# Gated mix of sliding-window attention and a SwiGLU block: two tiles' gate and up products moved into the block products, and the inverses of the softmax sums moved into the last slots

## The chip, the cores and the metric

The kernel runs on one core of a Trainium2 chip. The metric is the device time of one execution in microseconds (us). TensorE (PE, with its weight loads PEld), VectorE (DVE), ScalarE (ACT) and GpSimd (POOL) compute; SyncE (SP), ScalarE and GpSimd start transfers, which sixteen DMA engines carry out. Each engine works through its instructions in the order in which the program wrote them; nothing reorders them here.

## The reference

```python
def _A_ref(x, wqkv, wo):              # S = 2048, D = 512, H = 32 heads of 16, W = 256
    qkv = (x @ wqkv).reshape(B, S, 3, H, Dh).transpose(2, 0, 3, 1, 4)
    scores = einsum("bhqd,bhkd->bhqk", q, k) * (Dh ** -0.5)
    mask = (i - j >= 0) & (i - j < W)
    p = softmax(where(mask, scores, -1e9)); o = einsum("bhqk,bhkd->bhqd", p, v)
    return o.transpose(0, 2, 1, 3).reshape(B, S, D) @ wo
def _B_ref(x, w_gate, w_up, w_down):  # F = 1792
    return (silu(x @ w_gate) * (x @ w_up)) @ w_down
g = sigmoid((x * gate_w).sum(-1))
return g * _A_ref(x) + (1 - g) * _B_ref(x)
```

All is float32. The kernel gets float32 accuracy out of TensorE by splitting each operand into a high half (`hi`, a cast on ScalarE) and a low half (`lo`, a subtraction on VectorE or GpSimd), and by three matmuls per product (`split`, L66; `mm3`, L76).

## The kernel before, in words

The work has four stages, and TensorE passes through them without a break.

**Values and block products (to L439).** First the inputs are loaded: `x` by chunks of 512 tokens and `wv`, alternately on SyncE's queue (L143 to L148). Then the value projection of all 16 token blocks (L209). Then `PAIRS` (L149): the query and key projections of two head groups at a time, as seven block products of a Strassen-Winograd scheme (`product`, L357) in place of eight, for both halves of the tokens (`a`). A pair is 7 x 2 x 6 = 84 matmuls of 128x512. Each result block is handed to `put_c` (L332), which splits it and writes it to DRAM (`xd`); `stack` (L317) reads it back in the layout that the scores need. `soon` puts a step off by a number of products.

**First scores (L629 to L656).** 64 ticks in which the row maxima of group 0 are found.

**Slots (L734 to L770).** 128 slots `t`, 16 for each of the 8 head groups `g`; each has four ticks `hd`, one a head. A tick runs one matmul of `stage1` (L533: scores of group g+1 for the row maxima, taken by VectorE, L547), one of `stage2` (L573: scores of group g, exponential on ScalarE, L586, masks on GpSimd, L588 and L591) and a number of steps of `stream` (L526). Two score banks each (`ps1`, `ps2`) lie between TensorE and VectorE or ScalarE. In the last group (from t = 112, `g7`) there is no `stage1`, and `stage2` runs two heads in every second tick. Every fourth slot, after its second tick, holds a value product (`av`, L596, up to 96 short matmuls), then `evacuate` (L613): ScalarE and VectorE copy its two banks, GpSimd adds and writes to `od`. The sum of the softmax comes out of the same product, as one more column.

`stream` computes gate and up of the SwiGLU block, 14 tiles of 128 columns with two products each: 28 `UNITS`, for each 48 steps. A step is two matmuls of 64 rows side by side (`lanes`, L476; `whole`, L500, for the first unit). A unit's four result blocks are copied by ScalarE (L516) and written to `raws` (L517); its weights are split by ScalarE and GpSimd (`prepare`, L296). 192 steps run beside the first scores, 1152 in the slots: 9 a slot. How many steps a tick gets is written out by hand (L754 and L762).

Single steps are attached to ticks by `at(k, ...)`, `later(n, ...)` and `spread`, with k = 4t + hd; they run at the end of their tick. So are placed: the gate (`gate_block`, L661: load a block of x, multiply and sum on VectorE nine ticks later; `gate_end`, L667); early loads of `wd` (L673); early loads and the silu of the first SwiGLU tiles (`tile_load`, L683; `tile_early`, L688; `tile_silu`, L700), for which the freed query and key slots serve (`pieces`).

**The tail (L772 to L954).** 56 tiles (four token chunks c of 14 tiles n): load gate and up from `raws` (`load_kept`), silu and product (`hidden`), halves (`halved`), 12 matmuls with `wd` (`step`). Beside it the attention output: `load_oc` reads the unnormalized heads of a chunk from `od`, `load_den` the softmax sums, `put_den` inverts them on VectorE and writes `rd`, `load_rd` reads the inverses back, spread over the heads' rows; `attn_step` divides, splits and multiplies by `wo`. In the tail of the kernel before, all four `load_den` stand at its beginning, `put_den` at tiles 9 to 12 of chunk 0, the reads of chunk 0 at tiles 10 to 13 and those of chunk c at its first four tiles. All of these transfers are GpSimd's. Chunk 0's division begins at tile 1 of chunk 1.

Of the kernel before, what the change touches and what calls it, by code (L numbers as in the profile page):

```python
# [33 lines left out]
def gated_mix(ctx, tc, xT, xn, wqk, wv, wo, wgu, wd, gw, out):  # L34
# [70 lines left out]
    UNITS = [("f", f, i) for f in range(NF) for i in range(2)]  # L105
# [37 lines left out]
    for k in range(NK):  # L143
        nc.sync.dma_start(xk(0, k), xT[0, k])
        nc.sync.dma_start(wvraw[k], wv[:, k])
# [3 lines left out]
    PAIRS = [(("p", g), ("p", g + 1)) for g in range(0, G, 2)]  # L149
    RW = {0: pair_fetch(PAIRS[0])}  # L150

# [297 lines left out]
    with ExitStack() as A:  # L449
# [207 lines left out]

        gwb = osb.tile([P, D], F32, name="gwb")
        nc.sync.dma_start(gwb, gw[None, :].to_broadcast([P, D]))

        def gate_block(b):  # L661
            t = osb.tile([P, D], F32, name="xn", bufs=2)
            nc.sync.dma_start(t, xn[b * P:(b + 1) * P])
            later(9, lambda: nc.vector.scalar_tensor_tensor(t, t, 1.0, gwb, op0=ALU.mult, op1=ALU.mult,
                                                            accum_out=gate[:, b:b + 1]))

        def gate_end():  # L667
# [3 lines left out]
            nc.vector.tensor_scalar(igate, gate, -1.0, 1.0, op0=ALU.mult, op1=ALU.add)  # L671

# [64 lines left out]

        for t in range(G * NB + 1):
# [5 lines left out]
            for hd in range(4):  # L744
# [9 lines left out]
                n = (2, 1, 2, 2)[hd] if values else (k + 1) * 9 // 4 - k * 9 // 4  # L754
# [15 lines left out]
        run(last_tile)  # L770

    with ExitStack() as B:  # L772
# [26 lines left out]

        DEN = wop.tile([P, NCH, P], F32, name="den")  # L800
        shares = od.rearrange("g (j e) s -> (g j) e s", e=32)[:, DH]

        def load_den(c):
            nc.gpsimd.dma_start(DEN[:, c], shares[:, c * CH:(c + 1) * CH].rearrange("h (q i) -> h q i", q=4))

        def put_den(c):
            nc.vector.reciprocal(DEN[:, c], DEN[:, c])
            nc.gpsimd.dma_start(rd[c].rearrange("h (q i) -> (h q) i", q=4), DEN[:, c])

# [99 lines left out]
        for c in range(NCH):  # L909
            load_den(c)  # L910
        GOT[0, 3] = GOT[3]
        loads = seq[4:]
# [3 lines left out]
        for c, n in seq[3:]:  # L916
# [5 lines left out]
            if c == 0:  # L922
# [5 lines left out]
                else:  # L928
# [5 lines left out]
                    if n >= 10:  # L934
                        load_oc(0, n - 10)
            elif n < 4:
                load_oc(c, n)
            if c == 0 and n >= 10:
                load_rd(0, n - 10)
            elif c and n < 4:  # L940
                load_rd(c, n)
# [47 lines left out]
```

## Time and profile before

| what | us |
|---|---|
| median of three runs (lowest, highest) | 835.11 (833.59, 836.22) |
| the profiled execution's own time | 835.55 |
| its span, first to last instruction | 833.8 |
| TensorE busy in it | 816.1 |
| value projection and head pairs end at | 127.45 |
| first slot begins at, last value product ends at | about 182, about 621 |

The profile is one execution as the chip's profiler took it. Busy time counts an engine's instructions; an engine off the critical path may idle for nothing. A row of a timeline gives start, duration, engine, line, operation, written and read tile and shape; brackets give the idle time before it and what ended that. Matmuls are pipelined, so their durations overlap; the distance between starts is what one costs.

### The profile page before, as it was taken

The numbers are of one execution on the slowest core, as the hardware profiler recorded it, in microseconds if no ns is written. First come the engines' busy times: TensorE is split into PE (matmuls) and PEld (weight loads), VectorE is DVE, ScalarE is ACT, GpSimd is POOL, SyncE is SP. The second block draws the span as 40 slices with busy tenths as digits, with TensorE's granted clock in tenths as the row PEclk, the third lists the DMA queues.
The fourth block names the chain that finished last, engine by engine and source line by source line (L and its number), as shares of the span: only waits on it lengthen the run. The fifth ranks groups of instructions, "written<-read, shape, count | busy, mean of one in ns | idle before, by whom it ended". The sixth has DMA issues, their size and how long they took to land.

```text
span 833.8 us, 20786 instructions
## 1 busy us (share of the span) xinstructions
PE 816.1 (98%) x7897; PEld 684.0 (82%) x7897; DVE 541.6 (65%) x1394; ACT 471.0 (56%) x953; POOL 398.7 (48%) x712
## 2 busy tenths in 40 slices
PE   8999999999999999999999999999999979999997
PEld 7888887998888888888888888888887768888886
DVE  5675534877868787778787777783477466365462
ACT  7454552246767676666666766676776433434341
POOL 5124468035656575656565665665734532123220
PEclk9999999999999999999999999999999979999999
DMA  8446668672555556466446543534559995685741
GB/s 292 151 161 242 227 253 290 222 225 94 178 164 179 174 179 204 136 202 209 149 167 192 175 159 130 191 107 146 204 191 361 256 220 160 190 263 167 220 146 51
DMA packets 80420, 158.94 MB, mean 191 GB/s; under 512 B 14912, under 2 KB 19392, under 8 KB 80320
## 3 DMA queue, kind: packets, MB, share of 16 engines
q1 hardware_dynamic: 70128, 130.32, 48.7%
q0 software_dynamic: 10192, 27.29, 10.2%
q8 instruction: 62, 1.02, 0.5%
q14 instruction: 38, 0.31, 0.1%
HBM read 92.80 MB, written 64.75 MB: 189 GB/s over the span
## 4 chain that ended last, share of the span: by engine, by line
PE 88%; DMA 5%; DVE 4%; POOL 1%; ACT 1%; issue 1%; SPq 0%; DVEq 0%; ACTq 0%; POOLq 0%
PE pa L489 17%; PE pb L489 17%; PE ps L608 9%; PE ps L545 6%; PE ps L584 5%; PE ps L82 5%; PE ps L81 5%; PE ps L80 4%; PE ps L371 4%; PE pa L371 3%; PE ps L209 3%; PE pb L371 3%; DVE ps L547 2%; PE pb L81 2%; PE pb L80 2%; DMA got<-raws 2%
## 5 line engine op out<-in xcount | busy, mean ns | idle before, releaser
L547 DVE CUSTOM_DVE_ANT_0 ps<-ps,mask 128x384 f32<-128x384 f32 (+2 forms) x512 | 272.6, 545 | 50.2 <-PE ps L545 24.0
L586 ACT ACTIVATE pt<-ps 128x384 f32<-128x384 f32 (+2 forms) x512 | 237.2, 478 | 83.0 <-PE ps L545 31.9
L584 PE MATMUL ps<-q,k 64*128 64x384 f32 (+2 forms) x512 | 165.5, 333 | 0.1
L545 PE MATMUL ps<-k,q 63*128 63x384 f32 (+2 forms) x512 | 159.2, 331 | 1.9 <-DVE mx L547 0.4
L588 POOL TENSOR_SCALAR_AFFINE_SELECT pt<-pt 128x256 f32<-128x256 f32 x256 | 107.0, 418 | 107.0 <-ACT pt L586 102.4
L545 PEld LDWEIGHTS ps<-k,q 63*128 63x128 f32 x512 | 88.9, 184 | 20.4 <-DVE mx L547 10.1
L584 PEld LDWEIGHTS ps<-q,k 64*128 64x128 f32 x512 | 93.1, 184 | 9.9 <-ACT pt L586 4.4
L489 PE MATMUL pb<-xhi,wh 64*128 64x512 f32 x432 | 98.8, 402 | 0.0
L489 PE MATMUL pb<-xlo,wh 64*128 64x512 f32 x432 | 97.2, 393 | 0.0
L489 PE MATMUL pa<-xhi,wh 64*128 64x512 f32 x432 | 96.7, 399 | 0.0
L489 PE MATMUL pb<-xhi,wl 64*128 64x512 f32 x432 | 96.5, 392 | 0.0
L489 PE MATMUL pa<-xlo,wh 64*128 64x512 f32 x432 | 95.2, 393 | 0.0
L489 PE MATMUL pa<-xhi,wl 64*128 64x512 f32 x432 | 94.4, 392 | 0.0
L591 POOL TENSOR_SCALAR_AFFINE_SELECT pt<-pt 128x256 f32<-128x256 f32 x224 | 93.0, 415 | 0.0
L608 PE MATMUL ps<-pt,vg 64*32 64x320 f32 (+4 forms) x2816 | 77.0, 348 | 0.2
L862 DVE TENSOR_TENSOR sg<-got,sg 128x512 f32<-128x512 f32 x52 | 45.1, 866 | 47.3 <-ACT sg L861 35.6
L608 PEld LDWEIGHTS ps<-pt,vg 64*32 64x32 f32 x2816 | 51.7, 106 | 26.8 <-issue 9.7
L547 DVE DVE_READ_ACCUMULATOR2_ANT mx<- 128x1 f32 x512 | 72.5, 142 | 0.0
L626 POOL TENSOR_TENSOR oe<-oe,ob 128x512 f32<-128x512 f32 (+1 forms) x28 | 35.3, 1262 | 54.1 <-ACT ob L619 50.4
L625 DVE COPY oe<-ps 128x512 f32<-128x512 f32 x28 | 19.4, 692 | 60.0 <-issue 43.5
L489 PEld LDWEIGHTS pb<-xhi,wh 64*128 64x128 f32 x432 | 50.9, 185 | 5.2 <-issue 3.2
L71 POOL TENSOR_TENSOR ol<-raw,oh 128x512 fp32r<-128x512 f32 x16 | 22.5, 1409 | 67.0 <-ACT oh L68 66.8
(246 smaller groups left out, 1717.0 us busy)
## 6 DMA issues: line engine op xcount, KB each, us to landing
raws<-ev SPq DMA_DIRECT2D x112, 256.0 KB
got<-raws SPq DMA_DIRECT2D x104, 256.0 KB
q<-xd SPq DMA_DIRECT2D x96, 128.0 KB
k<-xd SPq DMA_DIRECT2D x96, 128.0 KB
xd<-cx SPq DMA_DIRECT2D x16, 512.0 KB
xd<-cy SPq DMA_DIRECT2D x16, 512.0 KB
od<-oe POOLq DMA_DIRECT2D x32, 256.0 KB, 3.1
raw<-wgu SPq DMA_DIRECT2D x28, 256.0 KB
```

The costliest lines, as they stand in the source:

```text
L80: nc.tensor.matmul(ps, lh, rh, start=start and i == 0, stop=False, skip_group_check=skip)
L81: nc.tensor.matmul(ps, lh, rl, start=False, stop=False, skip_group_check=skip)
L371: nc.tensor.matmul(ps, l[:, w], r[:, k], start=n in (1, 2, 5) and k == m == 0, stop=k == 1 and m == 2, skip_group_check=True)
L489: mm = nc.tensor.matmul(ps[me], w[r], x[r], start=not second and i == 0, stop=bool(second) and i == n - 1)
L545: nc.tensor.matmul(ps[:, :n], QT[g % 2][pr][r, q0:q0 + P], KT[g % 2][pr][r, k0:k0 + n], start=True, stop=True)
L547: mx = nc.vector.tensor_tensor_reduce(out=ps[:, :n], in0=ps[:, :n], in1=mask[:, 3 * P - n:], scale=1.0, scalar=NEG, op0=ALU.add, op1=ALU.m ...
L584: nc.tensor.matmul(ps[:, :n], KT[g % 2][pr][r, k0:k0 + P], QT[g % 2][pr][r, k0:k0 + n], start=True, stop=True)
L586: BEHIND.append(nc.scalar.activation(pt[:, j, :n], ps[:, :n], AF.Exp, scale=SCALE))
L588: nc.gpsimd.affine_select(out=pt[:, :, :P], in_=pt[:, :, :P], pattern=[[0, 2], [1, P]], compare_op=ALU.is_ge, fill=0.0, base=0, channel_mu ...
L591: nc.gpsimd.affine_select(out=pt[:, :, 2 * P:], in_=pt[:, :, 2 * P:], pattern=[[0, 2], [-1, P]], compare_op=ALU.is_ge, fill=0.0, base=-1, ...
L608: nc.tensor.matmul(AV[g, c][h][32 * j:32 * j + 32, q0 - c * CH:q1 - c * CH], VG[4 * g + kb // 4][o, kb % 4, 17 * j:17 * j + 32], PT[g, kb, ...
L862: nc.vector.tensor_tensor(out=sg, in0=gu[1], in1=sg, op=ALU.mult)
```

## The change

- `NSF = 2`: gate and up of tiles 0 and 1 leave `UNITS` and become two more entries of `PAIRS`, after the head pairs. `put_c` then writes their result blocks to `raws` in float32, without halves; a block that still lies in PSUM is copied by ScalarE first. The last pair, beside which the constant rows are set and group 0's stacks are read, is now one of these.
- The slots get 60 steps for eight slots (7.5 a slot) in place of 72. In the slots with a value product it is 2, 1, then 1 behind the product, then 1, 2.
- The loads of `wv` at the start go to ScalarE's queue.
- The gate's operation on VectorE is no longer due nine ticks after its load but is collected in `UNDER` and issued between a value product and its evacuation. `gate_end` moves from slot 110 to 114.
- The inverses: `invert(c)` reads the sums of chunk c in the slot after its last value product and inverts them six ticks later, for chunks 0 to 2; for chunk 3 all of it runs at once behind the last slot. The tail's `load_den` and `put_den` go.
- Tile loads and `tile_early` come earlier, and `tile_early` advances every tick (one tick is left out between the two tiles) in place of every second one.
- The tail's reads of heads and inverses come from one list, from tile 4 on: one a tile up to tile 19, then every second tile, then two in three.

```diff
+    NSF = 2
+    UNITS = [("f", f, i) for f in range(NSF, NF) for i in range(2)]
...
-        nc.sync.dma_start(wvraw[k], wv[:, k])
+        nc.scalar.dma_start(wvraw[k], wv[:, k])
...
+    PAIRS += [(("f", f, 0), ("f", f, 1)) for f in range(NSF)]
...
+        if PAIRS[p][r][0] == "f":
+            if psum:
+                t = c_tile()[:, 0].bitcast(F32)
+                nc.scalar.copy(t, src)
+                src = t
+            soon(1, lambda: nc.sync.dma_start(raws[PAIRS[p][r][1], r, c], src))
+            return
...
-            later(9, lambda: nc.vector.scalar_tensor_tensor(t, t, 1.0, gwb, op0=ALU.mult, op1=ALU.mult,
-                                                            accum_out=gate[:, b:b + 1]))
+            UNDER.append(lambda: nc.vector.scalar_tensor_tensor(t, t, 1.0, gwb, op0=ALU.mult, op1=ALU.mult,
+                                                                accum_out=gate[:, b:b + 1]))
...
+        def invert(c):
+            den = osb.tile([P, P], F32, name="den")
+            nc.gpsimd.dma_start(den, shares[:, c * CH:(c + 1) * CH].rearrange("h (q i) -> h q i", q=4))
+            yield
+            nc.vector.reciprocal(den, den)
+            nc.gpsimd.dma_start(rd[c].rearrange("h (q i) -> (h q) i", q=4), den)
+            yield
...
-            at(4 * (18 + 4 * b) + 2, lambda b=b: gate_block(b))
-        at(4 * (g7 - 2), gate_end)
+            at(4 * (17 + 4 * b) + 2, lambda b=b: gate_block(b))
+        at(4 * (g7 + 2), gate_end)
+        INV = [invert(c) for c in range(NCH)]
+        for c in range(NCH - 1):
+            for n in range(2):
+                at(4 * (g7 + 5 + 4 * c) + 2 + 6 * n, lambda c=c: run(INV[c], 1))
...
-            at(4 * (g7 + 9) + 3 + 2 * n, lambda n=n: tile_load(n, RAW_AT[n]))
+            at(4 * (g7 + 9) + 1 + n, lambda n=n: tile_load(n, RAW_AT[n]))
...
-            at(4 * (g7 + 10) + 3 + 2 * n, lambda: run(early, 1))
-        at(4 * (g7 + 13), lambda: tile_load(2, RAW_AT[2]))
-        at(4 * (g7 + 15) + 3, lambda: tile_load(3, RAW_AT[3]))
+            at(4 * (g7 + 10) + 2 + n + n // 6, lambda: run(early, 1))
+        at(4 * (g7 + 12) + 2, lambda: tile_load(2, RAW_AT[2]))
+        at(4 * (g7 + 14) + 2, lambda: tile_load(3, RAW_AT[3]))
...
+        STEPS = 60
...
-                n = (2, 1, 2, 2)[hd] if values else (k + 1) * 9 // 4 - k * 9 // 4
+                n = (2, 1, 1, 2)[hd] if values else (k + 1) * STEPS // 32 - k * STEPS // 32
...
                     av(*divmod(d - 1, NCH))
+                    while UNDER:
+                        UNDER.pop(0)()
                     evacuate(*divmod(d - 1, NCH))
                     if t < G * NB:
-                        run(steps, 2)
+                        run(steps, STEPS // 8 - 6)
...
         run(last_tile)
+        run(INV[3])
...
+        shares_due = [lambda f=f, c=c, k=k: f(c, k) for c in range(NCH) for k in range(NK) for f in (load_oc, load_rd)]
...
-                    if n < 13:
-                        ready.pop(0)()
-                        put_den(n - 9)
+                elif n < 13:
+                    ready.pop(0)()
...
+            m = NF * c + n
+            if m >= 4 and (m < 20 or (m % 2 == 0 if m < 36 else m % 3 != 2)) and shares_due:
+                shares_due.pop(0)()
```

More of the change, by code (lines that the diff above doesn't have):

```diff
@@ L103, in weights_of @@
         return wqk[key[1]] if key[0] == "p" else wgu[key[1], :, key[2]]
-    UNITS = [("f", f, i) for f in range(NF) for i in range(2)]
+    NSF = 2
+    UNITS = [("f", f, i) for f in range(NSF, NF) for i in range(2)]
     pp = ctx.enter_context(tc.tile_pool(name="pp", bufs=2, space=PSUM))
@@ L656, in gated_mix @@
         put_max(0, 1)
+        UNDER = []
         gwb = osb.tile([P, D], F32, name="gwb")
@@ L671, in gate_end @@
             nc.vector.tensor_scalar(igate, gate, -1.0, 1.0, op0=ALU.mult, op1=ALU.add)
+        shares = od.rearrange("g (j e) s -> (g j) e s", e=32)[:, DH]
+        def invert(c):
[5 more added lines that the diff above has]
+            yield
         def wd_early(k, f, piece):
@@ L798, in load_oc @@
             nc.gpsimd.dma_start(OC[c][:, k], heads[:, :DH, c * CH:(c + 1) * CH])
[L800 to L808, printed above, removed]
         RD = [t.bitcast(F32) for c in range(2, 4) for t in (xhi[c], xlo[c])]
@@ L908, in gated_mix @@
         ready = [load_wo(k) for k in range(3)]
-        for c in range(NCH):
-            load_den(c)
         GOT[0, 3] = GOT[3]
+        shares_due = [lambda f=f, c=c, k=k: f(c, k) for c in range(NCH) for k in range(NK) for f in (load_oc, load_rd)]
         loads = seq[4:]
```

9 lines of the change are left out of this document (removed).

## The prediction

> **What bounds the kernel now.** I read the page first, then busy time by stretches, then the idle rows of TensorE.
>
> ```profile
> PE 816.1 (98%) x7897; PEld 684.0 (82%) x7897; DVE 541.6 (65%) x1394; ACT 471.0 (56%) x953; POOL 398.7 (48%) x712
> PE 88%; DMA 5%; DVE 4%; POOL 1%; ACT 1%; issue 1%; SPq 0%; DVEq 0%; ACTq 0%; POOLq 0%
> ```
>
> TensorE is busy for 98% of the span and carries 88% of the chain that ended last. So time goes away where its instructions go away or where it stands idle, and comes back where another engine makes it wait. Three stretches from the busy times by stretch (from:to and length in us; then busy time of PE, PEld, DVE, ACT, POOL; granted clock; DMA share; GB/s):
>
> ```profile
> 294.00:350.00 56.00, 55.57 (x769) 46.18 (x767) 42.93 (x144) 38.13 (x83) 33.55 (x72) 1.00 0.57 179
> ...
> 660.00:670.00 10.00, 5.02 (x23) 3.82 (x21) 0.09 (x1) 3.60 (x6) 2.35 (x4) 0.87 1.07 239
> 670.00:680.00 10.00, 8.14 (x24) 6.49 (x25) 8.19 (x10) 3.68 (x7) 4.36 (x4) 0.62 1.06 232
> ```
>
> In the slots (first row, groups 2 and 3) TensorE is full; VectorE has 13 of 56 us to spare, ScalarE 18. From 660 to 680 the DMA engines are full (1.07, 1.06) and TensorE has a hole:
>
> The timeline of TensorE there (start, duration, then the instruction, and in brackets the idle time before it and its releaser):
>
> ```profile
> 664.63 0.39 PE L81 MATMUL ps<-q,hh 128*128 128x512 f32 x1
> 671.86 0.80 PE L82 MATMUL ps<-q,hl 128*128 128x512 f32 x1 [6.84 <-DVE hl L71]
> ```
>
> It idles 6.84 us. The granted 0.87 means 2.6 us at half clock in the first ten, 0.62 means 7.6 us in the second: half clock from 667.4 to 677.6, beginning 2.4 us after the last matmul ended (665.02). TensorE worked 5.7 us of it at half speed, which lost 2.9. The hole costs 9.7.
>
> [...]
>
> **The sum, part by part** (us, against the profiled execution's own 835.55, of which 833.8 are span; the median of the three runs, 835.11, is 0.44 below it).
>
> *Block products: +38.1.* A pair of the first stage today, as a stretch:
>
> ```profile
> 70.33:89.37 19.04, 19.04 (x86) 15.77 (x85) 10.39 (x16) 9.77 (x18) 8.36 (x7) 1.00 0.68 249
> ```
>
> 84 matmuls in 19.04, no idle, every other engine at 56% or less. Two pairs more are 2 x 19.04. Their copies to `raws` are cheaper than the halves of a head pair (no GpSimd work), so I add nothing; SyncE gets 16 writes of 256 KB for the 16 that leave the slots. If a result tile came free too late, it would show as a wait of a product.
>
> *Steps that leave the slots: -44.7.* Three starts of score matmuls, one tick apart:
>
> ```profile
> 503.88 0.34 PE L545 MATMUL ps<-k,q 63*128 63x384 f32 x1
> 504.52 0.34 PE L584 MATMUL ps<-q,k 64*128 64x384 f32 x1
> 505.39 0.33 PE L545 MATMUL ps<-k,q 63*128 63x384 f32 x1
> ```
>
> The first tick has two steps (0.64), the second three (0.87): 0.23 a step, 0.17 for the two score matmuls. 4 units x 48 = 192 steps x 0.233 = 44.7. Of these 168 lie in groups 0 to 6 (39.1), 24 in the last group (5.6). The block products are 6.6 cheaper than the steps they replace; all else is what the slots do with it.
>
> *Crowding in groups 0 to 6: +8.4.* An average tick falls from 0.70 to 0.61 us. What it has to cover:
>
> ```profile
> 439.68 0.57 DVE L547 CUSTOM_DVE_ANT_0 ps<-ps,mask 128x384 f32<-128x384 f32 x1
> ...
> 440.27 0.57 DVE L547 CUSTOM_DVE_ANT_0 ps<-ps,mask 128x384 f32<-128x384 f32 x1
> ```
> ```profile
> 477.33 0.60 ACT L516 COPY ev<-pb 128x512 f32<-128x512 f32 x1
> 477.80 0.53 ACT L586 ACTIVATE pt<-ps 128x384 f32<-128x384 f32 x1
> 478.18 0.65 ACT L68 CAST wh<-raw 128x512 fp32r<-128x512 f32 x1
> ```
>
> VectorE's timeline, then ScalarE's. Maxima follow each other at 0.59, so two-step ticks (0.64) still fit, and only one tick in sixteen has one step without a value product near. ScalarE needs 0.38 for an exponential, 0.47 for a copy, 0.51 for a cast. At each unit's end two copies and a cast come in three ticks: 3 x 0.38 + 2 x 0.47 + 0.51 = 2.6 against 1.9. Two score banks hide some 0.4 of it; I count 0.17 for each of 18 units, 3.0. The sure part stands behind each value product:
>
> ```profile
> 514.49 0.69 DVE L625 COPY oe<-ps 128x512 f32<-128x512 f32 x1 [2.49 <-issue]
> ```
> ```profile
> 514.53 0.59 ACT L619 COPY ob<-ps 128x512 f32<-128x512 f32 x1 [1.57 <-PE ps L608]
> ```
> ```profile
> 514.30 0.50 PE L489 MATMUL pa<-xhi,wh 64*128 64x512 f32 x2
> ```
>
> VectorE and ScalarE copy from 514.49 and 514.53; TensorE's first step after the product starts at 514.30. The evacuation frees the product's bank at about 515.24; head 3's scores need that bank. Today four steps and two score matmuls stand before them (about 515.4), afterwards two steps (515.04): 0.2 late, 27 times, 5.4. Bounds: 0 if the banks come free sooner than I read them, 16 if every unit pays the whole 0.7.
>
> *Gates under the value products: -4.9.* Starts of value products on the chain, four periods apart, and the gate operation:
>
> ```profile
> 343.98 2.48 PE ps L608 x95
> 400.35 2.51 PE ps L608 x95
> 511.85 2.52 PE ps L608 x95
> 566.99 2.48 PE ps L608 x95
> ```
> ```profile
> 305.76 0.69 DVE L664 SCALAR_TENSOR_TENSOR xn<-xn,gwb 128x512 f32<-128x512 f32 x1
> ```
>
> 56.37 with four gate blocks, 55.14 with none: 0.31 a block, 16 blocks. The operation (0.69) fits into the 2.48 in which VectorE has at most one maximum left; behind it stands the evacuation, which waits for the product anyway. Bounds 0 and -6.
>
> *The last group gives back 7.6.* Its scores come in pairs:
>
> ```profile
> 597.75 0.87 ACT L586 ACTIVATE pt<-ps 128x384 f32<-128x384 f32 x2 [0.22 <-PE ps L584]
> 599.08 0.87 ACT L586 ACTIVATE pt<-ps 128x384 f32<-128x384 f32 x2 [0.45 <-PE ps L584]
> ```
> ```profile
> 603.27 0.57 DVE L692 TENSOR_SCALAR ev<-ev 128x512 f32<-128x512 f32 x1 [3.75 <-ACT ev L691]
> 603.87 3.35 DVE L693 RECIPROCAL ev<-ev 128x512 f32<-128x512 f32 x1
> 607.26 0.84 DVE L694 TENSOR_TENSOR ev<-k,ev 128x512 f32<-128x512 f32 x1
> ```
>
> A pair takes 1.33 where TensorE's own work is 4.5 steps and 0.17, 1.22: the exponentials (0.87 and about 0.45 from matmul to exponential) bind. With 3.75 steps TensorE needs 1.05, the exponentials hardly less; I take 1.27, so 32 pairs gain 1.9 of 5.6 (3.7 given back). Then the early tiles: from a tile's exponential to its cast ScalarE waits for addition, reciprocal and two products, 0.57 + 3.35 + 2 x 0.84 = 5.6, plus the steps from engine to engine. Ten ticks between them become five (3.2), and an inverse goes ahead of the reciprocal, 0.94 and its read. ScalarE stands at the cast with the exponentials queued behind, TensorE stops when both score banks are full. At tile 0 the value product covers most: I get 1.8 of idle; tile 1, with an evacuation before it in VectorE's queue, 2.7; less 0.5 that the short last slots make good, 4.0. The tile loads go out one to three slots earlier on SyncE; the last group leaves it time. Each inverse's read also holds GpSimd's queue until the group's write has landed, with mask selects behind it; these are needed only two slots later. Bounds of this part: 0 to 13.
>
> *The share reads: -9.7.* The hole at 665 waits for the first attention block (VectorE's L820), whose `rd` stands at the end of inverses, writes and sixteen reads that the code starts only at tiles 9 to 17. Afterwards three of four inverses exist already and the first chunk's eight reads go out from tile 4 to 11; needed at tile 15. Bounds 0 and -10.2.
>
> *The last inverse: +8.0.* It runs directly behind the last slot, and VectorE's queue stands at it. The page's row of the write it needs (median us to landing last), and today's timeline of GpSimd, then of TensorE; then, from the view of the tile `den`, the landing of its transfers and its reciprocal:
>
> ```profile
> od<-oe POOLq DMA_DIRECT2D x32, 256.0 KB, 3.1
> ```
>
> ```profile
> 622.97 0.56 POOL L627 DMA_DIRECT2D od<-oe  x1 [4.46 <-DVE oe L621]
> ...
> 630.84 2.17 POOL L804 DMA_DIRECT2D den<-od  x4 [2.87 <-DMA od<-oe]
> ```
> ```profile
> 630.79 0.50 PE L80 MATMUL ps<-q,hh 128*128 128x512 f32 x1 [1.14 <-ACT hh L68]
> 632.09 0.50 PE L82 MATMUL ps<-q,hl 128*128 128x512 f32 x1 [0.57 <-DVE hl L71]
> ```
> ```profile
> DMA to landing us min/median/max: 3.1/5.1/8.3
> ```
> ```profile
> L807 DVE RECIPROCAL den<-den x4: 937/940/947, 642.2 to 650.0; 128x128 f32<-128x128 f32 x4
> ```
>
> The write of `od` is seen landed at 630.84, the read takes 3.1 to 5.1 more, the reciprocal 0.94; behind it in VectorE's queue stands tile 3's product (0.69), then ScalarE's cast (0.60): 636.3 to 638.3. TensorE has three tiles ready and is through with them at 629.65; today it lost 1.7 there. So about 5.3 more idle, and with an idle over 2.4 half clock from 632.0 to 642.2, worked in from 636.8: 2.7. Also behind it, on GpSimd: the last inverse's write, then `wo` and all share reads, with six tiles to spare. Bounds: 2 (the write lands early) to 12. [...]
>
> *The start: -1.5.*
>
> ```profile
> 1.26 0.41 SPq L145 DMA_DIRECT2D u<-wv  x1
> ```
> ```profile
> 8.35 0.62 ACT L68 CAST wvh<-u 128x512 fp32r<-128x512 f32 x1 [0.93 <-DMA u<-wv]
> 8.99 0.62 ACT L68 CAST xhi<-q 128x512 fp32r<-128x512 f32 x1
> ```
> ```profile
> 10.38 0.50 PE L209 MATMUL pa<-wvl,xhi 128*128 128x512 f32 x1 [0.86 <-POOL wvl L71]
> ```
>
> Half the issues move to ScalarE (nearest price 0.41 each). TensorE's waits before 10.4 come to about 2, all for first loads; the same work could start up to that much earlier, or 0.5 later if ScalarE's table load waits behind its four issues. [...]
>
> Sum: 38.1 - 44.7 + 8.4 - 4.9 + 7.6 - 9.7 + 8.0 - 1.5 = +1.3. From 835.55 that is 836.9, and 0.4 lower against the median: **836.5**. What one removes, another gives back.
>
> **Rivals.** *No crowding* (0.17): VectorE's and ScalarE's spare time in the slots absorbs all, and the early tiles' casts wait under the value products. For it: runs of four two-step ticks show no stall today. Without 8.4 and 4.0: 824. *The last inverse is hidden* (0.13): the write lands 3.1 us after its issue as half of them do, and TensorE's three tiles cover the rest: 828.5. *Slower: the clock falls in the last group* (0.17): at the casts of tiles 0 and 1. It decides at an idle of 2.4 us; my 1.8 and 2.7 lie on both sides. Each fall costs 10.2 us at half, 5.1, so up to 846.7. Against it: 1.14 us, quoted above, is the longest idle before 660 today. [...] *The reads do not come one a tile* (0.08): GpSimd issues them as soon as nothing blocks it, the DMA engines fill again (they moved 239 GB/s at 1.07) and the hole stays: 846.
>
> **Chances.** The forecast's case has 0.40 and its own range 832 to 841; 0.05 is left for others. A measurement of this kernel can tell 0.3% (2.5 us) from no change. Faster: the two fast rivals and 0.05 of the forecast's case, 0.35. Slower: the two slow ones, 0.12 of the forecast's case and 0.04, 0.41. The same: 0.24. Range 822 to 848: it takes in all four rivals and leaves the corners where several bounds meet.
>
> **What would show it.** Right: pairs at 19.04; value products about 12.3 apart without idle over 0.3; no gate operation between maxima; ScalarE waiting at L68 in the last group; a hole of 6 to 8 us about 8.5 us after the last value product, with a dip of the clock; none at the first attention tiles. Wrong: VectorE done with the last inverse before TensorE's third tile, or a second fall of the clock.

## The result, and the profile after

The changed kernel takes **849.29 us** (median of four runs, 847.60 to 850.33); the kernel before takes 835.23 beside it (833.59 to 836.22). The ratio is 1.0168, with a 95% interval of 1.0145 to 1.0192: slower by 14 us. The profiled execution took 850.33, with a span of 848.6.

TensorE's busy time first (the page after, part 1):

```profile
PE 826.2 (97%) x7681; PEld 673.8 (79%) x7681; DVE 555.6 (65%) x1420; ACT 471.5 (56%) x955; POOL 395.6 (47%) x708
```

It executes 216 matmuls fewer and is busy 10 us longer, so this row cannot say where the time went: from the first value product to the first of the last group the matmuls themselves wait for only 4.3 us, while their weight loads (PEld) wait for other engines for 29.3 us (rows below). The boundaries of the stages can say it. Starts on TensorE's timeline before (first block product, first unit, first value product, the first of the last group, the last one, first tail matmul), then the same six after:

```profile
51.13 0.39 PE L371 MATMUL pa<-xhi,ah 128*128 128x512 f32 x1
...
127.29 0.39 PE L505 MATMUL pa<-xhi,wh 128*128 128x512 f32 x1
...
190.73 0.50 PE L608 MATMUL ps<-pt,vg 64*32 64x320 f32 x8
...
566.92 0.50 PE L608 MATMUL ps<-pt,vg 64*32 64x320 f32 x8
...
618.72 0.50 PE L608 MATMUL ps<-pt,vg 64*32 64x320 f32 x8
...
621.20 0.50 PE L80 MATMUL ps<-q,k 128*128 128x512 f32 x1
```
```profile
50.77 0.39 PE L380 MATMUL pa<-xhi,ah 128*128 128x512 f32 x1
...
165.01 0.39 PE L514 MATMUL pa<-xhi,wh 128*128 128x512 f32 x1
...
227.54 0.50 PE L617 MATMUL ps<-pt,vg 64*32 64x320 f32 x8
...
581.85 0.49 PE L617 MATMUL ps<-pt,vg 64*32 64x320 f32 x7
...
636.21 0.50 PE L617 MATMUL ps<-pt,vg 64*32 64x320 f32 x8
...
638.70 0.50 PE L80 MATMUL ps<-q,k 128*128 128x512 f32 x1
```

| stretch | before | after | difference | forecast |
|---|---|---|---|---|
| start, to the first block product | 51.13 | 50.77 | -0.4 | -1.5 |
| block products | 76.16 | 114.24 | +38.1 | +38.1 |
| first scores, first four slots | 63.44 | 62.53 | -0.9 | -1.4 |
| 27 value-product periods of groups 0 to 6 | 376.19 | 354.31 | **-21.9** | **-34.2** |
| last group, four periods | 51.80 | 54.36 | +2.6 | +2.0 |
| last value product to the end of the span | 215.1 | 212.4 | -2.7 | -1.7 |

The forecast for the 27 periods is -37.7 (162 steps of 0.233, the rest of the 168 lies before the first value product), +8.4 of crowding and -4.9 for the gates. The differences add up to the span's +14.8 against the forecast's +1.3, and 12.3 of the 13.5 between them lie in this one line.

What TensorE waited for there is in the waits of its weight loads, from the first value product to the first of the last group (total us, times, longest). After:

```profile
PEld ps L554 <- DVE oe L634: 10.2, 27, 0.4
PEld ps L593 <- ACT pt L595: 6.7, 32, 0.5
PEld ps L617 <- issue: 6.5, 16, 0.8
PEld ps L617 <- POOL pt L597: 6.4, 11, 1.1
PEld ps L554 <- DVE mx L556: 6.0, 29, 0.3
```

L554 and L593 are the two score matmuls, L617 the value product; "issue" is time for which the profile shows no cause. Head 3's scores wait for VectorE's evacuation in each of the 27 periods; second-stage scores wait for exponentials, value products for GpSimd's masks.

### The profile page after: what moved, and what is told of

The parts are those of the page before. It is cut to its first block, busy times and chain, and to the rows that moved or that the text cites. A ratio compares the mean times of both kernels' runs of the same rounds, so it can differ in the third digit from the quotient of the medians.

```text
span 848.6 us, 20406 instructions
## 1 busy us (share of the span) xinstructions
PE 826.2 (97%) x7681; PEld 673.8 (79%) x7681; DVE 555.6 (65%) x1420; ACT 471.5 (56%) x955; POOL 395.6 (47%) x708
## 5 line engine op out<-in xcount | busy, mean ns | idle before, releaser
L556 DVE CUSTOM_DVE_ANT_0 ps<-ps,mask 128x384 f32<-128x384 f32 (+2 forms) x512 | 271.3, 544 | 38.0 <-PE ps L554 19.9
L593 PE MATMUL ps<-q,k 64*128 64x384 f32 (+2 forms) x512 | 175.8, 352 | 4.7 <-ACT pt L595 4.2
L554 PE MATMUL ps<-k,q 63*128 63x384 f32 (+2 forms) x512 | 162.5, 337 | 0.3
L554 PEld LDWEIGHTS ps<-k,q 63*128 63x128 f32 x512 | 88.8, 184 | 30.2 <-DVE oe L634 10.2
L593 PEld LDWEIGHTS ps<-q,k 64*128 64x128 f32 x512 | 93.8, 185 | 20.9 <-ACT pt L595 16.8
L498 PE MATMUL pa<-xhi,wh 64*128 64x512 f32 x368 | 85.8, 405 | 0.0
L498 PE MATMUL pa<-xhi,wl 64*128 64x512 f32 x368 | 85.7, 398 | 0.0
L498 PE MATMUL pb<-xhi,wh 64*128 64x512 f32 x368 | 85.1, 403 | 0.0
L498 PE MATMUL pa<-xlo,wh 64*128 64x512 f32 x368 | 85.1, 398 | 0.0
L498 PE MATMUL pb<-xhi,wl 64*128 64x512 f32 x368 | 83.7, 394 | 0.0
L498 PE MATMUL pb<-xlo,wh 64*128 64x512 f32 x368 | 83.1, 395 | 0.0
L617 PE MATMUL ps<-pt,vg 64*32 64x320 f32 (+4 forms) x2816 | 76.8, 348 | 4.4 <-POOL pt L597 2.9
L617 PEld LDWEIGHTS ps<-pt,vg 64*32 64x32 f32 x2816 | 53.2, 106 | 30.0 <-issue 8.3
L635 POOL TENSOR_TENSOR oe<-oe,ob 128x512 f32<-128x512 f32 (+1 forms) x28 | 35.2, 1256 | 55.7 <-ACT ob L628 51.1
L68 ACT CAST hh<-sg 128x512 fp32r<-128x512 f32 x53 | 32.7, 616 | 46.4 <-PE ps L81 34.0
L628 ACT COPY ob<-ps 128x512 f32<-128x512 f32 (+1 forms) x32 | 18.3, 573 | 64.1 <-PE ps L617 64.1
```

The source lines that it names most:

```text
L498: mm = nc.tensor.matmul(ps[me], w[r], x[r], start=not second and i == 0, stop=bool(second) and i == n - 1)
L554: nc.tensor.matmul(ps[:, :n], QT[g % 2][pr][r, q0:q0 + P], KT[g % 2][pr][r, k0:k0 + n], start=True, stop=True)
L556: mx = nc.vector.tensor_tensor_reduce(out=ps[:, :n], in0=ps[:, :n], in1=mask[:, 3 * P - n:], scale=1.0, scalar=NEG, op0=ALU.add, op1=ALU.m ...
L593: nc.tensor.matmul(ps[:, :n], KT[g % 2][pr][r, k0:k0 + P], QT[g % 2][pr][r, k0:k0 + n], start=True, stop=True)
L617: nc.tensor.matmul(AV[g, c][h][32 * j:32 * j + 32, q0 - c * CH:q1 - c * CH], VG[4 * g + kb // 4][o, kb % 4, 17 * j:17 * j + 32], PT[g, kb, ...
```

## The experiments

Two measures are used. The time is a median against the kernel before on the same chip. The *slots* are the 27 periods of groups 0 to 6 in the profiled execution, from value product to value product. Executions of one kernel spread by 1 to 7 us, so a difference of 2 us is read from the slots and not from the times. Each kernel's slots are read from one execution, but they repeat well: three kernels with the same slots of 7.5 steps (the changed one and two that differ from it only behind these groups) have 354.3, 354.3 and 354.4, three with the same nine steps 372.1, 371.9 and 371.8.

The theory: with 7.5 steps TensorE's slots are as short as what the other engines need for theirs, and they make it wait. The rivals: the other edits in the slots cost the time; or the waits are single prices that add up.

### Nine steps a slot again; and the products alone

The first kernel is the changed one without the two tiles' block products, the second the kernel before with nothing but them.

```diff
-    NSF = 2
+    NSF = 0
...
-        STEPS = 60
+        STEPS = 72
```

> The changed kernel with nine steps a slot again: the first stage makes no gate and up block products, all else of the change stays. Theory: in groups 0 to 6 the slots of 7.5 steps are so short that VectorE, ScalarE and GpSimd set their pace, and some 20 us of the 39 that the steps leave come back as waits. Then the block products' 37.7 go, the slots of groups 0 to 6 grow only from 354 to about 371 (as before, less the gates' 4.9), the last group grows by about 1: 829 to 832. Rival: the time was lost to the other edits in these slots (gates under the value products, share reads, masks behind them). Then the slots without the blocks pay for them too, about 12 us more: 840 to 844.

> The kernel before with the block products alone: two tiles' gate and up move to the first stage, 7.5 steps a slot; gates, inverses, share reads and the early tiles' ticks stay as before. Theory (short slots pace on other engines): 835.2 + 37.7 for the products - about 17 in groups 0 to 6 - about 2 in the last group: 852 to 856. Rival (the waits came with the other edits): 835.2 + 37.7 - 39.1 + 8.4 - 1.9, about 840.

Measured: 836.99 (ratio 1.0020, 1.0002 to 1.0038) and 852.63 (1.0225, 1.0205 to 1.0244). The rows of busy time over the slots, nine steps, then after, then the products alone:

```profile
190.35:562.44 372.09, 372.04 (x5177) 316.42 (x5175) 284.40 (x949) 254.61 (x562) 230.85 (x478) 1.00 0.52 168
```
```profile
227.54:581.85 354.31, 349.20 (x4852) 280.62 (x4850) 284.73 (x949) 247.07 (x545) 225.73 (x475) 1.00 0.51 164
```
```profile
228.13:591.53 363.40, 352.89 (x4852) 277.69 (x4850) 287.13 (x952) 247.72 (x546) 222.59 (x475) 1.00 0.49 160
```

The slots decide for the theory: 372.1, where it said about 371 and the rival wanted 12 more; the other edits do no harm there. The second kernel came where the theory put it (852 to 856; the rival said 840). By TensorE's own price the slots after should take 372.1 - 162 x 0.233 = 334.3. They take 354.3. **20.0 us are lost**, and only with short slots. The products alone lose more still, 363.4: with the gates back between the maxima, 16 gate operations cost 9.1, against 4.1 (376.2 - 372.1) with nine steps. (The 4.1 is not for the gates alone: the kernel with nine steps also has 2, 1, 3, 1, 2 steps in a slot with a value product, where the kernel before has 2, 1, 2, 2, 2.) The first kernel's time is 5 above the 829 to 832 expected: 2 of it in the last group, which takes 57.3 (51.8 before, some 55 expected); its profiled execution took 833.70, and what the longer ones among the ten (832.55 to 839.13) spent, no trace shows.

The same view of waits with nine steps names what has come with the short slots:

```profile
PEld ps L617 <- issue: 8.4, 28, 0.4
PEld ps L554 <- DVE mx L556: 5.7, 21, 0.3
...
PEld ps L593 <- ACT pt L595: 1.3, 7, 0.2
```

After less nine steps: evacuation +10.2, masks +6.4, exponentials +5.4, maxima +0.3, issue -1.9. That is 20.4, near the 20.0 lost. The two need not agree so well, since a weight load can wait while earlier matmuls still run (after, 29.3 us of such waits for other engines stand beside 4.3 of the matmuls' own): in the other kernels below the same difference misses the loss by 1 to 4. So the list says where the waits stand, and only roughly what each of them costs.

### The three waits, one by one and together

```diff
-                n = (2, 1, 1, 2)[hd] if values else ...
+                n = (1, 1, 2, 2)[hd] if values else ...
```
```diff
-                        later(1 + m, lambda m=m: nc.scalar.copy(places[m], ps[m]))
-                        later(4 + m, lambda m=m: nc.sync.dma_start(raws[...], places[m]))
+                        later(1 + 3 * m, lambda m=m: nc.scalar.copy(places[m], ps[m]))
+                        later(4 + 3 * m, lambda m=m: nc.sync.dma_start(raws[...], places[m]))
```
```diff
-                later(3, prepare)
+                later(next(n for n in range(3, 20) if (NOW[0] + n) % 16 in range(2, 11)), prepare)
```

> The changed kernel with the value slot's steps at 1, 1, 2, 2 and one behind the value product, where it has 2, 1, 1, 2 and one: one step more between the product and head 3's scores, one less ahead of it. Theory: head 3's scores wait for VectorE's evacuation of the product's bank, 10.2 us in 27 value slots; a step of 0.23 more covers 6 of it: 842 to 845. Rival: VectorE's maxima pace these slots; the product then starts before head 0's maximum has freed its bank, the wait only changes its name: 848 to 850.

> The changed kernel with the two copies at a unit's end three ticks apart in place of one. Theory: the exponentials behind these copies hold score banks; the waits of second-stage scores for ScalarE, 6.7 us against 2.8 with nine steps a slot, fall by 2 to 4: 845 to 847. Rival: they do not come from the copies: 848.5 to 850.

> The changed kernel with the weight split of each unit moved to a tick at which no mask is due before a value product (ticks 2 to 10 of 16). Theory: GpSimd's 1.29 us split stands ahead of the masks that the product reads; 6.4 us of the product's waits name these masks, and 3 to 5 go: 844 to 846. Rival: the masks are late because the exponentials are, or the product then waits for VectorE's maximum: 848 to 850.

> The three moves together on the changed kernel: steps 1, 1, 2, 2 and one in the value slot, copies three ticks apart, the weight split at quiet ticks. Theory: the crowding of some 20 us in groups 0 to 6 is made of these three places and adds up: 10 to 14 go, 835 to 839. Rival: the slots of 7.5 steps are at the pace of VectorE's and ScalarE's total work, so that a wait removed in one place returns at the next: 845 to 849.

Measured: 847.98, 849.14, 849.07 and, together, 846.00 (1.0121, 1.0093 to 1.0148). The slots lose 0.9, 2.3, 1.2, and 5.2 together. Each wait moved did fall: evacuation from 10.2 to 5.2, exponentials from 6.7 to 3.8, masks from 6.4 to 2.2 (each read from 228 to 580 us). But with the steps moved, the value products' waits for masks rose from 6.4 to 11.8 and those of scores for maxima from 6.0 to 10.3. With all three:

```profile
PEld ps L554 <- DVE mx L556: 12.5, 60, 0.3
PEld ps L617 <- POOL pt L597: 11.9, 21, 0.9
PEld ps L554 <- DVE oe L634: 5.1, 26, 0.2
```

The rivals are right here for the greater part: a wait taken away returns at the next engine. The single moves add up among themselves (4.4, together 5.2), but to far less than the 20 us.

### VectorE's loop

Why it returns is in VectorE's groups, over the slots (busy, mean ns, then idle time just before them). First two rows of the kernel before, then the first of these with nine steps, then both after.

```profile
L547 DVE CUSTOM_DVE_ANT_0 ps<-ps,mask 128x384 f32<-128x384 f32 (+2 forms) x431 | 232.2, 545 | 31.0 <-PE ps L545 15.1 <-PE ps L584 6.5
...
L625 DVE COPY oe<-ps 128x512 f32<-128x512 f32 x27 | 18.7, 692 | 57.0 <-issue 43.5 <-POOL pt L591 9.8 <-PE ps L608 3.7
```
```profile
L556 DVE CUSTOM_DVE_ANT_0 ps<-ps,mask 128x384 f32<-128x384 f32 (+2 forms) x431 | 231.8, 545 | 38.2 <-PE ps L554 20.5 <-PE ps L593 7.7
```
```profile
L556 DVE CUSTOM_DVE_ANT_0 ps<-ps,mask 128x384 f32<-128x384 f32 (+2 forms) x431 | 230.9, 544 | 19.7 <-PE ps L554 10.3 <-PE ps L593 0.2
...
L634 DVE COPY oe<-ps 128x512 f32<-128x512 f32 x27 | 18.7, 691 | 48.0 <-issue 34.0 <-POOL pt L600 5.8 <-POOL wl L71 4.4
```

VectorE is busy 80% of the time (284.7 of 354.3). But 48.0 of its idle time stands before the evacuation, that is, under the value product, when no scores arrive. Only 19.7 stand between maxima. Sixteen maxima, the evacuation, the gates and this standstill make a loop of 354.3 - 19.7 = 334.6 in the slots (372.1 - 38.2 = 333.9 with nine steps); TensorE's own is 334.3. If so, two loops of the same length are joined by two score banks, and neither has anything left to catch up with. To shorten VectorE's loop alone, the maxima were taken over fewer columns:

```diff
-                mx = nc.vector.tensor_tensor_reduce(out=ps[:, :n], in0=ps[:, :n], in1=mask[:, 3 * P - n:], ...
+                mx = nc.vector.tensor_tensor_reduce(out=ps[:, n - P:n], in0=ps[:, n - P:n], in1=mask[:, 2 * P:], ...
```

> The changed kernel with shorter maxima: VectorE takes each maximum over the last 128 columns of a score block (its diagonal block) instead of all 384, so the shift of the exponentials is another; 0.57 us becomes about 0.29 a maximum. Theory: outside the value products VectorE stands idle for only 20 of the 354 us of groups 0 to 6; its own loop (evacuation, sixteen maxima, and standing still under the product) is as long as TensorE's, so each jitter of one is paid by the other. With short maxima VectorE runs ahead and 7 to 14 us come back: 835 to 842. Rival: the waits are single latencies (evacuation behind the product, exponential to mask to product, copies), and the maxima's length matters only where scores wait for a maximum, 6 us of which 5 are there with nine steps too: 845 to 849.

> The kernel with the three moves together, and with the same shorter maxima. Theory: with VectorE's loop short nothing but latencies is left, and with these moved too groups 0 to 6 come near TensorE's own 334 (nine-step slots' 372.1 less 162 steps of 0.233): from 349 to 336 to 340, a time of 834 to 838. Rival: the chain exponential, mask, value product holds them: 842 to 846.

Measured: 849.51 (1.0161, 1.0120 to 1.0202) and 838.13 (1.0034, 1.0016 to 1.0053). The slots: 350.2, which is 4.1 better (7 to 14 expected), and 341.3, which is 13.1 better, just above the 336 to 340 expected. The first of them shows no gain in time: its profiled execution took 844.25, the other three 849.36 to 850.82. Their mean granted clock was 0.990 to 0.992 against 0.994, which accounts for at most 1.7 to 3.4 us of that (the difference in the clock, times 849); where they spent the rest, in the slots or outside, no trace shows. So the 4.1 stands for one execution. The second kernel is clear in both measures. With the three moves, after and without short maxima the slots read:

```profile
227.82:576.90 349.08, 343.42 (x4852) 280.67 (x4850) 282.55 (x949) 245.43 (x545) 225.27 (x476) 1.00 0.51 166
```
```profile
226.99:568.25 341.26, 339.19 (x4853) 292.54 (x4851) 183.92 (x949) 243.58 (x545) 224.37 (x476) 1.00 0.53 170
```

Neither theory holds alone. Short maxima give 4.1 and the moves 5.2, both together 13.1 of the 20.0. With short maxima alone VectorE stands idle between maxima for 107.6 us:

```profile
L556 DVE CUSTOM_DVE_ANT_0 ps<-ps,mask 128x128 f32<-128x128 f32 x431 | 127.8, 299 | 107.6 <-PE ps L554 78.8 <-PE ps L593 25.6 <-PE pa L498 0.4
```

Its loop is then far below TensorE's (350.2 - 107.6 = 242.6), and 15.9 of the 20.0 are still lost. So VectorE's loop is one part of the cause and not all of it. That fits several chains of about the same length, where one is shortened and another still binds; which ones, the runs show only in part. The same test at nine steps, then the masks left out:

> The kernel with nine steps a slot and all else of the change, with maxima over 128 columns in place of 384. Theory: at nine steps TensorE sets the pace and VectorE's length is covered: groups 0 to 6 stay at 371 to 372, the time at 834 to 838. Rival (VectorE's maxima cost time at any slot length): 365 to 368 there, 828 to 832.

> The changed kernel without GpSimd's masks of the probabilities (the window's limits are then not applied to the value products). Theory (several latencies behind one another): the value product's 6.4 us of waits for masks go, and with them 3 to 6 of groups 0 to 6, from 354 to 348 to 351; evacuation and copies stay. Rival (VectorE's loop sets the pace): the product then waits for head 0's maximum, and the groups stay at 353 to 354.

> The kernel with the three moves and the short maxima, and without GpSimd's masks of the probabilities. Theory: of the 6.9 us that its groups 0 to 6 stand above TensorE's own 334.4 (341.3), the masks are 3 to 5: 336 to 338, a time of 832 to 836. Rival: the rest is evacuation and exponentials, or the removed steps were worth less than 0.233 to TensorE: 340 to 341, a time of 837 to 839.

Measured: at nine steps 832.82 (0.9951, 0.9932 to 0.9970) with slots of 369.7; without masks 847.63 (1.0132, 1.0107 to 1.0158) with 351.6; without masks, with the moves and short maxima, 832.49 (0.9958, 0.9943 to 0.9973) with 338.2:

```profile
227.03:565.22 338.19, 337.72 (x4852) 287.64 (x4850) 181.96 (x949) 243.73 (x545) 70.93 (x71) 1.00 0.53 172
```

At nine steps VectorE's length costs 2.4, more than the nothing that was expected and less than the rival. The masks alone are worth 2.7, a little less than the 3 to 6 expected, and 3.1 on top of the rest. The rival named the reason: without masks the value products wait for maxima in their place (10.6 us in 26 waits, where the masks had cost 6.4). In the last kernel 3.9 of the 20.0 are left; waits of weight loads for the evacuation (5.5), the exponentials (3.9) and, at the value product, the first maxima (8.0) still stand there, partly covered by matmuls in progress. They were not taken apart further.

### One tile instead of two

```diff
-    NSF = 2
+    NSF = 1
...
-        STEPS = 60
+        STEPS = 66
```

with the two edits of the next part.

> One tile's gate and up as block products, 8.25 steps a slot, otherwise as the fastest kernel so far (old ticks for the early tiles, last inverse in the tail). Theory: crowding begins only where TensorE's slots come near VectorE's loop (some 12.4 a period); at 8.25 steps TensorE has 13.1, so of the 19 us that the products cost the slots give back 18 less some 4: 831 to 835 against 828.8. Rival: crowding grows from nine steps on in proportion: 10 of the 18 are lost, 838 to 841.

Measured: 832.54 (0.9949, 0.9927 to 0.9972), as the theory had it. The slots:

```profile
208.90:567.63 358.73, 358.30 (x5013) 300.83 (x5012) 282.40 (x949) 251.48 (x555) 230.44 (x477) 1.00 0.52 167
```

TensorE's own price would be 372.1 - 81 x 0.233 = 353.2: 5.5 lost at 8.25 steps, 20.0 at 7.5. The crowding is not in proportion to the steps: the first half of the cut costs 5.5, the second 14.5.

### The end of the slots and the tail

TensorE's idle times after, with what ended them:

```profile
624.24 0.82 PE L593 MATMUL ps<-q,k 64*128 64x384 f32 x2 [2.65 <-ACT pt L595]
...
632.53 0.66 PE L593 MATMUL ps<-q,k 64*128 64x256 f32 x2 [1.30 <-ACT pt L595]
...
652.63 0.80 PE L80 MATMUL ps<-q,hh 128*128 128x512 f32 x1 [5.48 <-ACT hh L68]
```

The first two are the early tiles, the third is behind the last inverse, as the timelines of GpSimd, VectorE and ScalarE show:

```profile
645.13 0.54 POOL L687 DMA_DIRECT2D den<-od  x1 [4.17 <-DMA od<-oe]
```
```profile
650.43 0.95 DVE L689 RECIPROCAL den<-den 128x128 f32<-128x128 f32 x1 [9.72 <-DMA den<-od]
651.30 0.63 DVE L880 TENSOR_TENSOR sg<-q,sg 128x512 f32<-128x512 f32 x1
```
```profile
651.96 0.62 ACT L68 CAST hh<-sg 128x512 fp32r<-128x512 f32 x1 [5.79 <-DVE sg L880]
```

```diff
-        run(INV[3])
...
+        den3 = wop.tile([P, P], F32, name="den3")
+        nc.gpsimd.dma_start(den3, shares[:, 3 * CH:].rearrange("h (q i) -> h q i", q=4))
...
                     if n == 9:
                         ready.append(load_wo(3))
+                        nc.vector.reciprocal(den3, den3)
+                        nc.gpsimd.dma_start(rd[3].rearrange("h (q i) -> (h q) i", q=4), den3)
```

> The changed kernel with the last share inverse put back into the tail: its read issued at the start of the tail, its reciprocal and write at the first chunk's tile 9; the other three stay in the last slots. Theory: the 5.48 us in which TensorE waits for a cast of the gate and up activation, and the half clock after it (3.4 us, 1.7 lost), are due to VectorE's queue standing at this inverse; about 7 go: 841 to 843. Rival: the activation's work behind the last slot is late by itself (addition, reciprocal, two products), the wait stays and the time is 848 to 850.

```diff
-            at(4 * (g7 + 9) + 1 + n, lambda n=n: tile_load(n, RAW_AT[n]))
+            at(4 * (g7 + 9) + 3 + 2 * n, lambda n=n: tile_load(n, RAW_AT[n]))
...
-            at(4 * (g7 + 10) + 2 + n + n // 6, lambda: run(early, 1))
-        at(4 * (g7 + 12) + 2, lambda: tile_load(2, RAW_AT[2]))
-        at(4 * (g7 + 14) + 2, lambda: tile_load(3, RAW_AT[3]))
+            at(4 * (g7 + 10) + 3 + 2 * n, lambda: run(early, 1))
+        at(4 * (g7 + 13), lambda: tile_load(2, RAW_AT[2]))
+        at(4 * (g7 + 15) + 3, lambda: tile_load(3, RAW_AT[3]))
```

> The changed kernel with the tile loads and the early tiles' steps at the ticks of before (every second tick in place of each). Theory: TensorE's idle times of 2.65 and 1.30 us in the last group come from ScalarE standing at the casts of tiles 0 and 1 with the exponentials queued behind, and the half clock after the first costs 1.7 more; with the old spacing they go: 843 to 845. Rival: with 7.5 steps the last group is bound by its exponentials and evacuations anyway, and what the casts cost shows up at another place: 848 to 850.

Measured: 848.78 (1.0169, 1.0146 to 1.0191) and 848.20 (1.0158, 1.0131 to 1.0184). Both theories fell by size: each wait goes and another takes its place. (The half clock behind the 5.48, put at 3.4 us there, lasted 6.8, from 650.56 to 657.39.) Without the last inverse the tail waits for transfers; ScalarE's timeline of that kernel, and its busy times with the DMA share (last column but one):

```profile
654.75 0.63 ACT L878 ACTIVATE sg<-got 128x512 f32<-128x512 f32 x1 [2.81 <-DMA got<-raws]
```
```profile
655.00:660.00 5.00, 3.64 (x17) 2.67 (x16) 1.89 (x3) 2.29 (x5) 0.00 (x0) 1.00 1.07 238
```

With GpSimd no longer held by the inverse, the first `wo` goes out at 643.37 in place of 652.61 and the first share read at 646.02 in place of 654.73. The DMA share is 1.01 to 1.07 from 645 to 660, and the gate and up tiles come late; that the former delay the latter is read from these rows and was not tested. With the old ticks the tail begins 3.4 earlier (635.33 against 638.70), but TensorE goes on only 1.6 earlier behind the last inverse (652.63 above), because the write of `od` that the inverse reads landed 7.0 us after its issue in place of 4.7:

```profile
651.08 0.80 PE L80 MATMUL ps<-q,hh 128*128 128x512 f32 x1 [7.29 <-ACT hh L68]
```

So in the changed kernel neither edit is worth undoing alone; there, both were not undone together. On the kernel with nine steps they were undone one after the other:

> Nine steps a slot, no gate and up block products, gates under the value products, share reads one a tile, and the early tiles' steps at the old ticks. Theory: the last group loses the 5.5 that the early tiles' casts cost there (57.3 against 51.8 before), groups 0 to 6 keep 372; but the last inverse then binds earlier, since its chain ends about 14 after the last value product: 828 to 832. Rival: nothing is gained, the inverse takes all of it: 835 to 838.

> As the kernel with nine steps and the early tiles at the old ticks, and the last inverse in the tail (its read at the tail's start, its reciprocal and write at tile 9). Theory: both the last group's 5.5 and the wait for the last inverse go, the DMA engines stay as full there as before: 824 to 829, faster than both kernels. Rival: as in the run that put only the inverse back, late reads of the gate and up tiles take the wait's place: 831 to 836.

Measured: 831.93 (0.9965, 0.9950 to 0.9980) and **828.76** (0.9927, 0.9905 to 0.9949), both in the range of the theory. The last group falls from 57.3 to 53.3, the wait at the tail's start from 6.6 with the inverse to 2.0 without it. Here the old ticks gain 5.1 by themselves (836.99 to 831.93) and the inverse 3.2 more:

```profile
628.55 0.50 PE L80 MATMUL ps<-q,hh 128*128 128x512 f32 x1 [2.02 <-ACT hh L68]
```

The last kernel is faster than both: it keeps from the change the loads of `wv` on ScalarE's queue, the gates under the value products, the three early inverses and the reads one a tile, and neither the block products nor the short slots.

## Why the prediction was wrong, point by point

- **Block products, +38.1:** right, 38.1.
- **Steps that leave the slots, -44.7:** nothing speaks against 0.233 a step as TensorE's price, but no run shows it bare. With short maxima, the moves made and the masks out, the slots are 33.9 of the 37.7 shorter than with nine steps (31.5 shorter than with nine steps and short maxima). How much of the rest is price and how much is waiting stays open. The 20.0 lost hang on this price.
- **Crowding in groups 0 to 6, +8.4: this step failed.** It was 20.0: two parts of the term were too small, and a third was missing. The evacuation was put at 5.4, and its waits were 10.2: from 514.30, two steps and two score matmuls at the sum's own prices end at 514.94 and not at 515.04, which is 0.3 late and 8.1 in all. The copies were put at 3.0; the waits for exponentials rose by 5.4, of which 2.9 went away with the copies moved. (By the sum's own figures, 0.7 less the 0.4 hidden is 0.3, and 5.4 in 18 units; and its upper bound of 16 would be 18 x 0.7 + 5.4 = 18.0.) The masks, 6.4 of waits, were not in the sum at all. That 8.1, 5.4 and 6.4 make 19.9 is no proof: with all three places moved only 5.2 came back.
- **Behind it stands the sentence that VectorE has 13 of 56 us to spare.** In the kernel before, 57.0 of its idle time in the slots lay under the value products, where no scores arrive. 31.0 lay between maxima (38.2 with the gates moved and nine steps), and 37.7 were to be taken from there. What VectorE's loop costs is shown by the pair of kernels with and without short maxima, 7.8 with the moves made and 4.1 without; the 5.5 at 8.25 steps fits it. It is a part of the 20.0.
- **Gates under the value products, -4.9:** 4.1 with nine steps, with the reservation above. In the short slots they are worth 9.1: there the waits of scores for maxima are 20.0 with the gates between the maxima and 6.0 without.
- **The last group gives back 7.6:** right in sum (+2.6 against -5.6 + 7.6 = +2.0), by luck in its parts. With the block products alone the last group takes 47.8, so the shorter slots save 4.0 there, where 1.9 was forecast. The other edits cost 6.5, where the early tiles' 4.0 was forecast. TensorE's idle times of 2.65 and 1.30 come to the 4.0; the fall of the clock behind the first, up to 1.7, was not in this term. With the old ticks the changed kernel's last group takes 48.2, though 2.4 of that gain come back as a wait in the last value product.
- **Share reads -9.7, last inverse +8.0:** together -2.2 against -1.7, up to TensorE's last matmul. The hole of 6.84 is gone (no idle time after 653 is above 1.23). The last inverse's hole came where it was forecast, 8.4 us behind the end of the last value product, but with 5.48 it was smaller than the 6 to 8: 3.8 more than the 1.7 lost there before, where the sum had 5.3. The half clock behind it (0.50 from 650.56 to 657.39), with 4.8 us in it from TensorE's first matmul on, cost 2.4 by half of that (2.7). That makes 6.2 in place of 8.0, and leaves some 8.4 for the share reads in place of 9.7. Undoing the inverse alone gave nothing clear of noise (ratio 1.0169 against 1.0168), since waits for transfers took its place; undoing it with the old ticks, at nine steps, gave 3.2.
- **The start, -1.5:** 0.4, at the edge of what the runs can tell: the first block product starts at 50.4 to 51.2 in the sixteen kernels with `wv` on ScalarE's queue, at 51.1 and 51.4 in the two without. ScalarE's table load (1.28 us) stood behind its four issues and began at 2.70 in place of 0.81, its first cast at 5.34 in place of 3.63.
- **The slower rival** (the clock falls in the last group, 846.7) is near the time measured, but not its cause: the clock did fall after the idle 2.65, but for 3.4 us (0.50 from 626.67 to 630.08) in place of 10.2, which costs at most 1.7 in place of 5.1.

## What to carry to other kernels

An engine's idle share is no measure of what it can take on: part of the idle time can lie where the engine has no work to do. Ask of each engine how long its own loop is without the idle time that it could use, counting the stretches in which it must stand still, and put that beside the bound engine's loop after the change. Where the two met here, a cut of 37.7 us paid back 17.7, and repairs of single waits moved them for the greater part. And where one wait stands in front of another, as in the changed kernel's tail, undoing one edit alone does not show what it costs.

## What the runs showed of the hardware

TensorE's granted clock read 1.00 or 0.50. The two stretches of 0.50 after and the one before, each with what lies around it (from:to and length, then busy times, and the clock in the third column from the end):

```profile
623.25:626.67 3.42, 2.19 (x11) 1.35 (x13) 1.73 (x4) 3.22 (x8) 0.85 (x3) 1.00 0.89 250
626.67:630.08 3.41, 3.41 (x19) 3.41 (x19) 3.38 (x2) 1.61 (x4) 2.32 (x7) 0.50 0.57 213
630.08:633.49 3.41, 2.11 (x19) 1.58 (x16) 2.12 (x3) 1.72 (x5) 1.88 (x4) 1.00 0.49 142
```
```profile
647.15:650.56 3.41, 0.01 (x1) 0.00 (x0) 0.13 (x1) 0.00 (x0) 0.00 (x0) 1.00 0.94 349
650.56:653.97 3.41, 1.22 (x3) 0.51 (x3) 3.32 (x6) 2.01 (x4) 1.90 (x4) 0.50 0.10 32
653.97:657.39 3.42, 3.42 (x8) 2.77 (x9) 3.42 (x6) 2.85 (x6) 3.42 (x7) 0.50 0.83 237
657.39:660.80 3.41, 3.41 (x16) 2.78 (x16) 3.14 (x6) 1.80 (x4) 0.34 (x1) 1.00 1.00 330
```
```profile
663.90:667.31 3.41, 1.12 (x5) 0.58 (x4) 0.00 (x0) 0.00 (x0) 0.95 (x2) 1.00 1.06 239
667.31:670.72 3.41, 0.00 (x0) 0.00 (x0) 0.81 (x2) 0.09 (x1) 0.00 (x0) 0.50 1.07 237
...
674.14:677.55 3.41, 3.41 (x9) 2.64 (x8) 3.41 (x5) 1.04 (x3) 1.61 (x1) 0.50 1.06 235
```

They lasted 3.41, 6.83 and 10.24 us. In the third, matmuls of 128x512 start 0.43 apart (674.16, 674.59, 675.01), behind it 0.23 (677.57, 677.80, 678.03). The first began 2.4 us after TensorE was at work again behind its idle 2.65 (624.24), the second 3.4 us after a matmul had ended (647.16), the third 2.3 after one had (665.02); TensorE was busy in them for 3.41, 4.64 and 5.69 us. So the idle time of 2.4 us and the 5.7 us of work that the prediction read from the third are figures of that stretch alone. How much work lay in the 3.41 us ahead does not decide it in these runs either: with short maxima the clock was 0.50 behind 1.32 us, after behind 2.19; with nine steps it was 1.00 behind 1.95, after behind 1.75 (619.84 to 623.25).

```profile
617.56:620.97 3.41, 1.32 (x8) 0.88 (x8) 1.65 (x3) 2.38 (x6) 0.77 (x2) 1.00 0.56 168
620.97:624.38 3.41, 3.22 (x16) 2.87 (x16) 3.34 (x3) 1.70 (x6) 2.03 (x5) 0.50 0.84 295
```
```profile
614.24:617.65 3.41, 1.95 (x17) 1.86 (x19) 2.03 (x3) 2.49 (x7) 0.80 (x2) 1.00 0.55 161
617.65:621.07 3.42, 3.42 (x62) 2.53 (x66) 0.03 (x1) 3.28 (x8) 1.31 (x3) 1.00 0.47 172
```

What makes the clock fall, and when it returns, was not shown.
